# Three pairs of taps of four columns added on VectorE, sums of exponentials in three parts, and the last copy split between two engines

## The chip, the cores and the metric

The kernel runs on one core of a Trainium2 chip. The core has a TensorE (PE in the profile, with its weight loads apart as PEld), a VectorE (DVE), a ScalarE (ACT), a GpSimd (POOL) and a SyncE (SP); each works through its own queue in order and they wait for each other through semaphores. The metric is device microseconds of one execution, lower is better. The median of the three runs shown is 405.34 us (405.34 to 405.47).

## The reference

Two stages over 8 sequences of 4160 tokens with 192 features. The first is a convolution whose seven weights differ for each token and each of eight heads; they come out of a softmax. The second multiplies with two matrices, takes the larger of the two results for each hidden feature, and multiplies back.

```
w = exp(weight_gen - max); w = w / sum(w)            # over the 7 taps, per token and head
x_pad = [6 zero tokens, x]
y[b,s,h,:] = sum over k of w[b,s,h,k] * x_pad[b, s+k, head h]
g = maximum(y @ w1, y @ w2)                          # 192 -> 1024
out = g @ w_out                                      # 1024 -> 192
```

## The kernel before, in words

**Tiling.** The 33280 tokens lie 260 to a partition; a token's place in its partition is called a column. The columns are cut into 17 batches (16 columns each, then one of 12 and one of 8), and a batch into units of 4 columns (batches 0 and 1) or 8 (after them; the last few are smaller again). There are 38 units. A unit of 4 columns starting at column 8 of batch 1 is unit 6: columns 24 to 27 in the kernel's order, "1.8" in the steps below.

**The softmax** of a batch takes these steps: `exp_sum` (`X`, L153, ScalarE) takes the exponentials, `red` (`n`, L168, VectorE) sums seven of them for each token and head, `ln` (`l`, L172, ScalarE) takes the logarithm of the sums, `shift` (`s`, L177, VectorE) subtracts it from the weights, and `weights` (`W`, L191, ScalarE) takes the exponential again. `red`, `ln` and `shift` work on a whole batch or on one of several parts of it; `part` gives the columns.

**The convolution.** `mul` (`m`, L211, VectorE) multiplies a unit's columns, shifted by each of the seven taps, with the weights into `m_t`. For units from 8 on `adds` sums the seven products on VectorE in three instructions: three pairs of taps (L227), two pairs (L233), the last pair (L236, into `y_t`). A transposing DMA (L245, issued by SyncE) then gives `yt`, which TensorE reads. For units 0 to 7 VectorE adds nothing: `sum_transpose` (`y`, L281) lets TensorE sum and transpose all seven products with 64-wide matmuls against an identity matrix (2 x 7 x 6 = 84 matmuls), and `sums_out` (`e`, L293, ScalarE) copies the sums out.

**The second stage.** It uses max(a, b) = a + relu(b - a). `hid_tile` (L336, TensorE) makes tiles of hidden differences in PSUM, `relu` (L346, ScalarE) moves them to SBUF, `out_first` (L388 and L376) and `out_second` (L376) form the result of some columns (TensorE), and `evac` (L434, ScalarE) copies the result out. `relay` is a ScalarE instruction between `out_first` and `out_second`: the latter starts when ScalarE's queue has come to it.

**Order.** Up to about 47 us a list written out by hand, `OPENING`, sets the order of all engines' queues. From then on the work goes by groups of three hidden tiles, numbered from 8, and `hidden` writes each group in this order: TensorE makes tiles a and b and does `out_first`; ScalarE does relu a, relu b, the relay; TensorE makes tile c; `before()`; ScalarE does relu c; TensorE does `out_second`; ScalarE does `evac`; `after()`. What `before()` and `after()` put into ScalarE's queue stands in the table `SOFTMAX_AT`: the key (16, 1) with "l.5" means that the logarithm of batch 5 comes after the evac of group 16, and (44, 1), (72, 0) hold l.10 and l.15. This table is not touched by the change.

VectorE's queue is written by `extra`: while TensorE works on the second half of batch b, VectorE multiplies and adds the second half of batch b+1, and beside these adds come the sums of exponentials of batch b+3, through the callback `beside(i, 3)`, which `adds` calls ahead of each of its three instructions (i = 0, 1, 2). Beside the adds of a batch's first half comes the `shift` of the following batch, in three parts. The sums are in two parts before the change: ahead of the first and of the second add.

**PSUM and buffers.** From group 8 on there is one PSUM tile each for hidden tiles a, b and c and one ("r") for the results: `out_first` of a group waits for the `evac` of the group before.

**The end.** `rest_of_results` makes the last results; for the very last pair of columns `evac` copies 2 x 192 numbers with one ScalarE instruction (L422) and sends them out with two DMAs (L425), one issued by ScalarE, one by SyncE.

Of the kernel before, what the change touches and what calls it, by code (L numbers as in the profile page):

```python
# [9 lines left out]
FP32 = mybir.dt.float32  # L10
# [7 lines left out]
def _sub(base: bass.AP, off: int, dims):  # L18
    ap = [list(base.ap[0])] + [[int(s), int(c)] for s, c in dims]
    return dataclasses.replace(base, offset=base.offset + off, ap=ap)  # L20
# [3 lines left out]
def kernel(  # L24
# [9 lines left out]
    nc = tc.nc  # L34

    B, S, D = x.shape
    H, K = weight_gen.shape[2], weight_gen.shape[3]
    F = moe_w1.shape[1]
    P = 128
# [3 lines left out]
    HF = F // 2  # L43
# [8 lines left out]
    NB = len(BATCHES)  # L52

    def dcol(c):

        return (c + ROT) % CPP


    def pieces(b):
        n = BATCHES[b][1]  # L60
        at, done = [], 0
        for w in (4, 4, 4, 4) if b < 2 else (8, 8) if n == 16 else (8, 4) if n == 12 else (4, 4):
            at.append((done, w))
            done += w
        return at
# [14 lines left out]
    consts = ctx.enter_context(tc.tile_pool(name="consts", bufs=1))  # L80
# [76 lines left out]
    def part(b, i, of):  # L157

        n = BATCHES[b][1]
        c0, c1 = (4 * i, n if i else 4) if of == FIRST else (n * i // of, n * (i + 1) // of)  # L160
        h0, h1 = c0 * H, c1 * H
        return slice(h0, h1), h0 * K, [[K, h1 - h0], [1, K]]

    def red(b, i=0, of=1):
        if i == 0:
            s_ts[b] = psm.tile([P, BATCHES[b][1] * H], FP32, name="sum_t", tag="sum")
        hs, at, ap = part(b, i, of)
        nc.vector.reduce_sum(out=s_ts[b][:, hs], in_=_sub(e_ts[b], at, ap), axis=AX.X)  # L168
# [48 lines left out]
    def adds(b, o, first=False, beside=lambda i, of: None):  # L217


        w = dict(pieces(b))[o]  # L220
        n = w * D

        def taps(at, step, cnt):
            return _sub(m_t, K * o * D + at * n, [[step * n, cnt], [1, w * D]])

        beside(0, 3)
        nc.vector.tensor_tensor(out=taps(0, 1, 3), in0=taps(0, 1, 3), in1=taps(3, 1, 3), op=ALU.add)  # L227
        if first:
            return
        beside(1, 3)  # L230
        if b not in y_ts:
            y_ts[b] = py.tile([P, 16 * D], BF16, name="y_t", tag="y")
        nc.vector.tensor_tensor(out=taps(0, 2, 2), in0=taps(0, 2, 2), in1=taps(1, 5, 2), op=ALU.add)  # L233
        beside(2, 3)

        nc.vector.tensor_tensor(  # L236
            out=_sub(y_ts[b], o * D, [[64, 2], [P, 3 * w // 2], [1, 64]]),
            in0=taps(0, 1, 1), in1=taps(2, 1, 1), op=ALU.add,
        )
# [24 lines left out]
    def half(j):  # L264
        return slice(64 * j, 64 * j + 64)


    LEFT = (0, 1, 2, K - 1)

    def sum_transpose(u, i=None):  # L270

        b, o, n = UNITS[u]
        assert n == 4
        to = "h" if i == 0 else "o"
        yps = yps_of[u, i] = ps[to].tile([P, 1024], FP32, name="yps", tag="hd" if i == 0 else "op")
        ks = range(6) if i is None else range(3 * i, 3 * i + 3)
        for k in ks:
            for t in range(K):
                at = K * o * D + (t * 6 + k if i is None else (K * i + t) * 3 + k % 3) * P
                for r in range(2):  # L280
                    nc.tensor.matmul(  # L281
                        yps[:, r * 512 + k * 64:r * 512 + (k + 1) * 64],
                        lhsT=m_t[half(r), at:at + P], rhs=ident[half(r), half(r)],
                        start=(k == ks[0] and t == 0), stop=(t == K - 1),
                        skip_group_check=True,
                    )
# [69 lines left out]
    def place(p):  # L356

        u, i, _ = column(2 * p)
        b, o, n = UNITS[u]
        return BATCHES[b][0] + o + i, n // 2  # L360
# [55 lines left out]
    def evac(p, n):  # L416

        tile_, at = op_at[p]
        o = o_t[0]
        if p == NT // 2 - 1:  # L420

            nc.scalar.copy(out=_sub(o_last, 0, [[D, 2], [1, D]]),  # L422
                           in_=_sub(tile_, at, [[512, 2], [1, D]]))
            for j, eng in enumerate((nc.scalar, nc.sync)):
                eng.dma_start(  # L425
                    out=bass.AP(tensor=out.tensor, offset=dcol(place(p)[0] + 2 * j) * D, ap=[[CPP * D, P], [1, D]]),
                    in_=o_last[:, j * D:(j + 1) * D],
                )
            return
        runs = [[q for q in range(p, p + n) if column(2 * q)[0] == u]  # L430
                for u in range(column(2 * p)[0], column(2 * (p + n - 1))[0] + 1)]
        for qs in runs:
            c, h = place(qs[0])
            copied = nc.scalar.copy(out=_sub(o, c % 24 * D, [[D, len(qs)], [h * D, 2], [1, D]]),  # L434
                           in_=_sub(tile_, at + (qs[0] - p) * D, [[D, len(qs)], [512, 2], [1, D]]))
        stores = []
        for q in range(p, p + n):
            u, i, _ = column(2 * q)
            if u == NU - 2 and UNITS[u][2] == 8 and i % 2:
                stores.append((nc.sync, place(q)[0] - 1, [4 * D, 2], [1, 2 * D]))  # L440
            elif u < NU - 1 and i == UNITS[u][2] // 2 - 1:
                w = i + 1
                for k in range(0, 2 * w, w if u in PARTED else 2 * w):
                    stores.append((nc.sync, place(q)[0] - i + k, [1, (w if u in PARTED else 2 * w) * D]))
            if u == NU - 1:
                stores.append((nc.sync, place(q)[0], [2 * D, 2], [1, D]))
        for eng, c, *ap in stores:

            def issue(eng=eng, c=c, ap=ap, o=o):
                eng.dma_start(  # L450
                    out=bass.AP(tensor=out.tensor, offset=dcol(c) * D, ap=[[CPP * D, P], *ap]),
                    in_=_sub(o, c % 24 * D, ap),
                )

            if 3 <= u < NU - 3:
                held.append(issue)
            else:
                while u > 3 and held:
                    held.pop(0)()
                issue()  # L460
        return copied
# [9 lines left out]
    for g in range(3, len(GROUPS)):  # L471
        most = 4 if g == 3 else 2 if GROUPS[g][1] == 2 or len(OUTS[-1]) == 4 else 4
        n = min(most, ready[g] - c)
# [69 lines left out]
    ident, swap = around[:, 0:P], around[:, 64:64 + P]  # L543
    zeros = consts.tile([P, PAD * D], BF16, name="zeros")
    gate = consts.tile([P, 1], FP32, name="gate")
    o_last = consts.tile([P, 2 * D], FP32, name="o_last")

    pstage = ctx.enter_context(ExitStack())
    stage = pstage.enter_context(tc.tile_pool(name="pstage", bufs=1))
# [2 lines left out]
    ws = {(kind, wi): stage.tile([P, w], FP32, name=f"ws{wi}{kind}") for kind, w in (("E", F), ("T", HF)) for wi in range(2)}  # L552
# [10 lines left out]
    def load_w(h, wi):  # L563

        wsrc = (moe_w1, moe_w2)[wi]
        return nc.sync.dma_start(
            out=ws["E", wi][:, h * HF:(h + 1) * HF],
            in_=bass.AP(tensor=wsrc.tensor, offset=h * HF, ap=[[F, P], [1, HF]]),
        )

    def load_last(h, wi):

        wsrc = (moe_w1, moe_w2)[wi]
        return nc.sync.dma_start(  # L574
            out=ws["T", wi][half(h), :],
            in_=bass.AP(tensor=wsrc.tensor, offset=P * F + h * HF, ap=[[F, 64], [1, HF]]),
        )
# [124 lines left out]
    def results_buffer(_):  # L702
# [22 lines left out]
        e.0.1 d.0 d.2 t.0 k.3 t.2 T.3 d.1 T.4 h.0 h.1 t.1 X.1 r.0 lx.0.8.4 T.1 lo.0 r.1 m.0.4 n.1 v.0 h.2  # L725
        lx.1.0.8 V.1 y.1 r.2 l.1 h.3 e.1 m.0.8 lg.2@l.1 s.1 V.0 m.0.12 r.3 h.4 W.1.0 m.1.0 y.2 h.5 r.4 p.0
        e.2 r.5 h.6 lx.1.8.8@r.4 lg.3@e.2 y.3 W.1.8 h.7 lh.2 C.1 C.0 C.2 A.3 W.1.4 X.2 r.6 e.3 B.3 m.1.4 h.8
        D.3 y.4 r.7 r.8 Z.0 E.3 n.2 X.3 l.2 m.1.8 A.4 e.4 W.1.12 lx.2.0.8.0@r.7 B.4 h.9 D.4 h.10 r.9 E.4 s.2
        r.10 lg.4@r.9 y.5 W.2.0 A.5 h.11 B.5 h.12 e.5 D.5 n.3 r.11 r.12 A.6 m.1.12 E.5 h.13 B.6 D.6 y.6 r.13
        E.6 h.14 e.6 l.3 lx.2.8.8@r.13 h.15 r.14 A.7 W.2.8 B.7 y.7 D.7 r.15 e.7 E.7  # L730
    """

    make_identity(nc, ident_f)
# [28 lines left out]
    def extra(t):  # L762

        u, k = TILES[t]
        b, o, n = UNITS[u]
        s = o + k

        if s == 0 and b + 1 < NB:
            mul(b + 1, 0)
        later = 0 if b < 4 else 5  # L770
        if s == later and b + 1 < NB:

            c = b + 1
            adds(c, 0, beside=lambda i, of: shift(c + 1, i, of) if c + 1 < NB else None)
        if s == 8 and b + 2 < NB:
            mul(b + 1, 8)
        if s == 8 + later and b + 2 < NB:
            adds(b + 1, 8, beside=lambda i, of: red(b + 3, i, 2) if b + 3 < NB and i < 2 else None)
        if s == 8 and b + 2 == NB:
            mul(b + 1, 4)  # L780
            adds(b + 1, 4)
        if k == n // 4 - 1 and 7 < u + 1 < NU:
            transpose(u + 1)

    def steps(g, tiles):

        for t in tiles:
            extra(t)
# [36 lines left out]
```

## Time and profile before

| what | us |
|---|---|
| median of three runs | 405.34 |
| the profiled execution's own time | 405.37 |
| span of its profile | 403.6 |
| TensorE busy in matmuls | 394.8 (98%) |
| VectorE busy | 369.1 (91%) |
| ScalarE busy | 360.9 (89%) |
| granted TensorE clock | 1.0 |
| ScalarE waits for VectorE's sums of exponentials | 0.2, once, at 5.4 |
| TensorE sums and transposes unit 6 | 41.97 to 43.19 |
| the last copy (L422) starts | 400.05 |
| its DMAs are issued; they land | 400.56; 402.42 and 402.59 |

The busy share of an engine says how much of the span it has an instruction running; it does not say whether the others wait for it. The timeline gives each instruction's start and duration in microseconds from the start of the span; consecutive records of one engine overlap by about 0.1 us, so what an instruction costs in a full queue is the distance between starts.

### The profile page before, as it was taken

The page shows a single profiled execution, that of the slowest core. Times are in us where ns is not written, and L with a number is a line of the kernel's source. Part 1 is how long each engine was busy: PE and PEld are TensorE (multiplying, and loading weights), DVE is VectorE, ACT ScalarE, POOL GpSimd, SP SyncE. Part 2 cuts the span into 40 slices and gives each one's busy share as a digit, 9 for nine tenths or more (in the row PEclk, how much of TensorE's full clock was granted, in tenths as well). Part 3 has the DMA queues.
Part 4 walks back from the last instruction along what each step waited for, and adds up shares of the span by engine and source line. Part 5 has one row for each costly group of instructions (what it writes and reads, how often), then busy time and mean ns, then how long its engine had stood idle before and what let it go on. Part 6 is the DMA issues. An engine that isn't in the chain of part 4 may idle for free.

```text
span 403.6 us, 16321 instructions
## 1 busy us (share of the span) xinstructions
PE 394.8 (98%) x7499; PEld 321.3 (80%) x7499; DVE 369.1 (91%) x211; ACT 360.9 (89%) x466; POOL 72.3 (18%) x96
## 2 busy tenths in 40 slices
PE   7799999999999999999999999999999999999996
PEld 3589999777778777778777778877777877787996
DVE  5999999999999999999999999999999999998200
ACT  5999899999999989999899999989999899888872
POOL 3111031211122210222220122122012121200000
PEclk9999999999999999999999999999999999999999
DMA  8956468767768646864766667777457847558304
GB/s 262 222 140 151 120 124 167 183 164 133 190 110 222 182 79 129 240 187 80 217 187 107 141 192 193 99 215 198 81 115 228 178 80 200 141 106 193 104 31 169
DMA packets 60883, 63.16 MB, mean 157 GB/s; under 512 B 47641, under 2 KB 48665, under 8 KB 60816
## 3 DMA queue, kind: packets, MB, share of 16 engines
q1 hardware_dynamic: 52816, 40.15, 36.4%
q0 software_dynamic: 7856, 21.89, 27.4%
q8 instruction: 58, 0.95, 1.0%
q10 hardware_dynamic: 144, 0.10, 0.1%
q14 instruction: 9, 0.07, 0.1%
HBM read 36.55 MB, written 25.56 MB: 154 GB/s over the span
## 4 chain that ended last, share of the span: by engine, by line
PE 92%; ACT 5%; DMA 1%; SPq 1%; issue 0%
PE op_ps L376 42%; PE hdc L336 13%; PE hdb L336 13%; PE hda L336 13%; PE op_ps L388 8%; ACT rd_t L346 2%; DMA ws0E<-in_moe_w_dram 1%; PE hdp L336 1%; PE yps L281 1%; ACT en_t L191 1%; ACT yt L293 1%; ACT e_t L153 0%; ACT w1t L644 0%; SPq L574 0%; ACT w L622 0%
## 5 line engine op out<-in xcount | busy, mean ns | idle before, releaser
L376 PE MATMUL op_ps<-wo,rd_t 64*128 64x192 bf16 x4160 | 210.6, 243 | 0.0
L376 PEld LDWEIGHTS <-rd_t 64*128 64x128 bf16 x4160 | 181.0, 94 | 14.7
L211 DVE TENSOR_TENSOR m_t<-xb,en_t 128x10752 bf16<-128x10752 bf16 (+2 forms) x39 | 187.8, 4821 | 1.5 <-ACT en_t L191 1.4
L336 PEld LDWEIGHTS <-wd 64*128 64x128 bf16 x1824 | 96.8, 94 | 40.4 <-issue 2.5
L346 ACT ACTIVATE rd_t<-hdc 128x1024 bf16<-128x1024 f32 x82 | 84.1, 1025 | 17.8 <-PE hdc L336 16.2
L253 POOL CAST gate<-yt 128x1 f32<-128x1 bf16 x30 | 39.9, 1332 | 271.3 <-DMA yt<-y_t 271.3
L346 ACT ACTIVATE rd_t<-hda 128x1024 bf16<-128x1024 f32 x81 | 83.4, 1030 | 0.2 <-ACT o_t L434 0.2
L346 ACT ACTIVATE rd_t<-hdb 128x1024 bf16<-128x1024 f32 x81 | 83.5, 1031 | 0.0
L227 DVE TENSOR_TENSOR m_t<-m_t 128x4608 bf16<-128x4608 bf16 (+1 forms) x30 | 73.0, 2433 | 0.1
L336 PE MATMUL hdc<-yt,wd 64*128 64x512 bf16 (+1 forms) x552 | 67.9, 353 | 0.0
L434 ACT COPY o_t<-op_ps 128x384 f32<-128x384 f32 (+1 forms) x99 | 56.1, 577 | 12.4 <-PE op_ps L376 12.3
L336 PE MATMUL hdb<-yt,wd 64*128 64x512 bf16 (+1 forms) x540 | 67.1, 355 | 0.0
L336 PE MATMUL hda<-yt,wd 64*128 64x512 bf16 (+1 forms) x540 | 67.1, 355 | 0.0
L388 PE MATMUL op_ps<-w,yt 64*128 64x192 bf16 x780 | 55.5, 243 | 0.0
L388 PEld LDWEIGHTS <-yt 64*128 64x128 bf16 x780 | 39.0, 94 | 14.5 <-issue 0.3
L233 DVE TENSOR_TENSOR m_t<-m_t 128x3072 bf16<-128x3072 bf16 (+1 forms) x30 | 50.2, 1674 | 0.1
L191 ACT ACTIVATE en_t<-wg_t 128x896 bf16<-128x896 f32 (+3 forms) x48 | 35.7, 773 | 3.0 <-PE op_ps L376 2.0
L236 DVE TENSOR_TENSOR y_t<-m_t 128x1536 bf16<-128x1536 bf16 (+1 forms) x30 | 27.5, 916 | 0.6
L177 DVE TENSOR_TENSOR wg_t<-wg_t,sum_t 128x280 f32<-128x280 f32 (+6 forms) x46 | 22.2, 483 | 0.0
L168 DVE TENSOR_REDUCE sum_t<-e_t 128x64 f32<-128x448 f32 (+3 forms) x31 | 19.7, 639 | 2.3 <-ACT e_t L153 2.3
L125 POOL DMA_DIRECT2D xb<-in_x_dram x34 | 18.2, 537 | 17.3 <-ACT rd_t L346 11.0
L153 ACT ACTIVATE e_t<-wg_t 128x896 f32<-128x896 f32 (+2 forms) x18 | 15.9, 886 | 2.1 <-DMA wg_t<-in_weight_gen_dram 2.1
(40 smaller groups left out, 110.0 us busy)
## 6 DMA issues: line engine op xcount, KB each, us to landing
out_dram<-o_t SPq DMA_DIRECT2D x21, 768.0 KB, 4.3
xb<-in_x_dram POOLq DMA_DIRECT2D x30, 384.0 KB, 5.0
out_dram<-o_t SPq DMA_DIRECT2D x22, 384.0 KB, 3.7
wg_t<-in_weight_gen_dram POOLq DMA_DIRECT2D x13, 448.0 KB, 5.7
xb<-xb POOLq DMA_DIRECT2D x7, 288.0 KB, 5.1
wg_t<-in_weight_gen_dram SPq DMA_DIRECT2D x2, 448.0 KB, 5.2
xb<-in_x_dram POOLq DMA_DIRECT2D x4, 192.0 KB, 6.4
xs<-in_x_dram SPq DMA_DIRECT2D x1, 576.0 KB, 4.3
```

What stands on the lines that cost most here:

```text
L177: nc.vector.tensor_tensor(out=w_t, in0=w_t, in1=_sub(s_ts[b], hs.start, [[1, hs.stop - hs.start], [0, K]]), op=ALU.subtract)
L191: act = nc.scalar.activation(out=_sub(en_ts[b], (o * WGC + ((i or 0) * J + j) * N * K) * 2, [[2 * N, K], [2, N], [1, 2]]), in_=_sub(wg_ts[ ...
L211: return nc.vector.tensor_tensor(out=m_out, in0=x_in, in1=_sub(en_ts[b], at * H * 2, [[2, K * n * H], [0, G // 2], [1, 2]]), op=ALU.mult,)
L227: nc.vector.tensor_tensor(out=taps(0, 1, 3), in0=taps(0, 1, 3), in1=taps(3, 1, 3), op=ALU.add)
L233: nc.vector.tensor_tensor(out=taps(0, 2, 2), in0=taps(0, 2, 2), in1=taps(1, 5, 2), op=ALU.add)
L236: nc.vector.tensor_tensor(out=_sub(y_ts[b], o * D, [[64, 2], [P, 3 * w // 2], [1, 64]]), in0=taps(0, 1, 1), in1=taps(2, 1, 1), op=ALU.add,)
L253: nc.gpsimd.tensor_copy(out=gate, in_=yt[:, 0:1])
L336: nc.tensor.matmul(hid_out(t, f, j), lhsT=wd_at(j, s, f // 4, f % 4 * P, P), rhs=_sub(yt_ts[u][half(j), :], (s + j) % 3 * P, [[3 * P, w // ...
L346: relu_of[t0] = nc.scalar.activation(out=rd[:, k * 1024:(k + n) * 1024], in_=hd[:, at:at + n * 1024], func=AF.Relu)
L376: return nc.tensor.matmul(op_out(c), lhsT=rd[rows, k * 1024 + at:k * 1024 + at + P], rhs=wo[rows, f * D:(f + 1) * D], start=False, stop=(r ...
L388: nc.tensor.matmul(op_out(c + j), lhsT=yt_ts[u][half(j), (3 * i + (s + j) % 3) * P:(3 * i + (s + j) % 3 + 1) * P], rhs=w10[half(j), s * D: ...
L434: copied = nc.scalar.copy(out=_sub(o, c % 24 * D, [[D, len(qs)], [h * D, 2], [1, D]]), in_=_sub(tile_, at + (qs[0] - p) * D, [[D, len(qs)] ...
```

## The change

Four things, in the order of the kernel's text:

- Unit 6: `OPENING` has a new step `a.1.8` behind `m.1.8`. It is `adds` with `first=True`: one VectorE instruction adds taps 3 to 5 to taps 0 to 2 for four columns. The unit is noted in `fewer`, and `sum_transpose` then lets TensorE sum four products (taps 0, 1, 2 and 6) in place of seven: 48 matmuls in place of 84.
- The last pair of columns: ScalarE copies the first 192 numbers, VectorE the second 192, each into its own tile, and each DMA waits for its own copy.
- The sums of exponentials beside the adds of a batch's second half come in three parts (5, 5 and 6 columns of 16) ahead of the three adds, in place of two parts (8 and 8) ahead of the first two.
- `load_w` and `load_last` get forms (both halves at once; an issue by ScalarE) that no step of `OPENING` calls.

```diff
@@ adds
         nc.vector.tensor_tensor(out=taps(0, 1, 3), in0=taps(0, 1, 3), in1=taps(3, 1, 3), op=ALU.add)
         if first:
+            fewer.add((b, o))
             return
@@ sum_transpose
+        taps = (0, 1, 2, K - 1) if (b, o) in fewer else range(K)
         for k in ks:
-            for t in range(K):
+            for t in taps:
@@ evac, the last pair of columns
-            nc.scalar.copy(out=_sub(o_last, 0, [[D, 2], [1, D]]),
-                           in_=_sub(tile_, at, [[512, 2], [1, D]]))
-            for j, eng in enumerate((nc.scalar, nc.sync)):
+            for j, (eng, copy) in enumerate(((nc.scalar, nc.scalar.copy), (nc.sync, nc.vector.tensor_copy))):
+                copy(out=o_last[j], in_=tile_[:, at + 512 * j:at + 512 * j + D])
                 eng.dma_start(
...
-                    in_=o_last[:, j * D:(j + 1) * D],
+                    in_=o_last[j],
@@ OPENING
-        D.3 y.4 r.7 r.8 Z.0 E.3 n.2 X.3 l.2 m.1.8 A.4 e.4 W.1.12 lx.2.0.8.0@r.7 B.4 h.9 D.4 h.10 r.9 E.4 s.2
+        D.3 y.4 r.7 r.8 Z.0 E.3 n.2 X.3 l.2 m.1.8 a.1.8 A.4 e.4 W.1.12 lx.2.0.8.0@r.7 B.4 h.9 D.4 h.10 r.9
+        E.4 s.2 r.10 lg.4@r.9 y.5 W.2.0 A.5 h.11 B.5 h.12 e.5 D.5 n.3 r.11 r.12 A.6 m.1.12 E.5 h.13 B.6 D.6
@@ extra
-            adds(b + 1, 8, beside=lambda i, of: red(b + 3, i, 2) if b + 3 < NB and i < 2 else None)
+            adds(b + 1, 8, beside=lambda i, of: red(b + 3, i, 3) if b + 3 < NB else None)
```

More of the change, by code (lines that the diff above doesn't have):

```diff
@@ L265, in half @@
         return slice(64 * j, 64 * j + 64)
-    LEFT = (0, 1, 2, K - 1)
+    fewer = set()
     def sum_transpose(u, i=None):
@@ L545 @@
     gate = consts.tile([P, 1], FP32, name="gate")
-    o_last = consts.tile([P, 2 * D], FP32, name="o_last")
+    o_last = [consts.tile([P, D], FP32, name=f"o_last{j}") for j in range(2)]
     pstage = ctx.enter_context(ExitStack())
@@ L565, in load_w, with load_last @@
         wsrc = (moe_w1, moe_w2)[wi]
+        at, w = (0, F) if h == 2 else (h * HF, HF)
         return nc.sync.dma_start(
-            out=ws["E", wi][:, h * HF:(h + 1) * HF],
-            in_=bass.AP(tensor=wsrc.tensor, offset=h * HF, ap=[[F, P], [1, HF]]),
+            out=ws["E", wi][:, at:at + w],
+            in_=bass.AP(tensor=wsrc.tensor, offset=at, ap=[[F, P], [1, w]]),
         )
-    def load_last(h, wi):
+    def load_last(h, wi, act=0):
         wsrc = (moe_w1, moe_w2)[wi]
-        return nc.sync.dma_start(
+        return (nc.scalar if act else nc.sync).dma_start(
             out=ws["T", wi][half(h), :],
@@ L727 @@
         e.2 r.5 h.6 lx.1.8.8@r.4 lg.3@e.2 y.3 W.1.8 h.7 lh.2 C.1 C.0 C.2 A.3 W.1.4 X.2 r.6 e.3 B.3 m.1.4 h.8
-        D.3 y.4 r.7 r.8 Z.0 E.3 n.2 X.3 l.2 m.1.8 A.4 e.4 W.1.12 lx.2.0.8.0@r.7 B.4 h.9 D.4 h.10 r.9 E.4 s.2
-        r.10 lg.4@r.9 y.5 W.2.0 A.5 h.11 B.5 h.12 e.5 D.5 n.3 r.11 r.12 A.6 m.1.12 E.5 h.13 B.6 D.6 y.6 r.13
-        E.6 h.14 e.6 l.3 lx.2.8.8@r.13 h.15 r.14 A.7 W.2.8 B.7 y.7 D.7 r.15 e.7 E.7
+        D.3 y.4 r.7 r.8 Z.0 E.3 n.2 X.3 l.2 m.1.8 a.1.8 A.4 e.4 W.1.12 lx.2.0.8.0@r.7 B.4 h.9 D.4 h.10 r.9
+        E.4 s.2 r.10 lg.4@r.9 y.5 W.2.0 A.5 h.11 B.5 h.12 e.5 D.5 n.3 r.11 r.12 A.6 m.1.12 E.5 h.13 B.6 D.6
+        y.6 r.13 E.6 h.14 e.6 l.3 lx.2.8.8@r.13 h.15 r.14 A.7 W.2.8 B.7 y.7 D.7 r.15 e.7 E.7
     """
```

## The prediction

> **What bounds the kernel now.** I read the page first, its busy shares and the chain that ended last.
>
> ```profile
> span 403.6 us, 16321 instructions
> ...
> PE 394.8 (98%) x7499; PEld 321.3 (80%) x7499; DVE 369.1 (91%) x211; ACT 360.9 (89%) x466; POOL 72.3 (18%) x96
> ...
> PE 92%; ACT 5%; DMA 1%; SPq 1%; issue 0%
> ```
>
> The reader is to see that TensorE is the bound: the chain runs on it for 92% of the span, and from about 30 us on it has no gap. So a matmul less is time won, and any wait that TensorE gets anew is time lost for good. The other two engines are at 89% and 91%, so neither has much room to make up a delay. Then the waits, for ScalarE's logarithms, since the change moves what they read.
>
> ```profile
> ACT sum_t L172 <- DVE sum_t L168: 0.2, 1, 0.2
> ```
>
> Of 18 logarithms only one ever waited for VectorE's sums, the one at 5.4 us. By the timelines the others have room, but unequal room: the change is decided there. Batch 5 has the least, on VectorE and on ScalarE:
>
> ```profile
> 80.20 0.61 DVE L168 TENSOR_REDUCE sum_t<-e_t 128x64 f32<-128x448 f32 x1
> 80.73 2.55 DVE L227 TENSOR_TENSOR m_t<-m_t 128x4608 bf16<-128x4608 bf16 x1
> 83.20 0.62 DVE L168 TENSOR_REDUCE sum_t<-e_t 128x64 f32<-128x448 f32 x1
> 83.72 1.75 DVE L233 TENSOR_TENSOR m_t<-m_t 128x3072 bf16<-128x3072 bf16 x1
> 85.51 0.96 DVE L236 TENSOR_TENSOR y_t<-m_t 128x1536 bf16<-128x1536 bf16 x1
> 86.39 5.75 DVE L211 TENSOR_TENSOR m_t<-xb,en_t 128x10752 bf16<-128x10752 bf16 x1
> ```
>
> ```profile
> 84.64 0.31 ACT L172 ACTIVATE sum_t<-sum_t 128x128 f32<-128x128 f32 x1
> 84.85 1.02 ACT L346 ACTIVATE rd_t<-hda 128x1024 bf16<-128x1024 f32 x1
> 85.75 1.03 ACT L346 ACTIVATE rd_t<-hdb 128x1024 bf16<-128x1024 f32 x1
> 86.75 1.02 ACT L346 ACTIVATE rd_t<-hdc 128x1024 bf16<-128x1024 f32 x1
> 87.67 0.47 ACT L434 COPY o_t<-op_ps 128x384 f32<-128x384 f32 x1
> ```
>
> The second part of the sums ends at 83.82 and l.5 starts at 84.64: 0.82 us of room. Behind l.5 in ScalarE's queue stand the relus, the relay and the evac of group 17, and TensorE waits for those.
>
> **The change part by part.**
>
> *Fewer matmuls.* In the chain the 84 matmuls of unit 6 take 1.22 us (41.97 to 43.19), 14.5 ns each. 36 go: 36 x 14.5 = 0.52 us. ScalarE's copy of these sums waits for them today (idle 0.49 ahead of it at 43.23), so ScalarE comes forward too, and the work up to 84 us moves forward by 0.52 on both engines. What is late next is looked at below.
>
> *The new add* (2304 numbers per partition). The same form stands near the end, behind a multiplication of the same size:
>
> ```profile
> 357.13 2.96 DVE L211 TENSOR_TENSOR m_t<-xb,en_t 128x5376 bf16<-128x5376 bf16 x1
> 360.12 1.36 DVE L227 TENSOR_TENSOR m_t<-m_t 128x2304 bf16<-128x2304 bf16 x1
> ```
>
> The multiplication holds the queue for 2.99 when the add needs its result, against 2.87 today (m.1.8 at 31.32, s.2 at 34.19). The add holds it for 1.36 less the 0.08 by which an independent successor starts early: 1.28. Together 2.99 - 2.87 + 1.28 = **1.40 us**, at 34 us. VectorE has no idle row from there to 363 us, so nothing swallows it: everything on VectorE comes 1.40 later. Near at hand this is covered: y.6 needs the add by 41.3, it is there at 35.6; W.2.0 starts at 36.90 and s.2 will end at 36.67; l.3 and m.2.0 have over 3 us and 2 us. The transposes have room too: the landing of `yt` leads its first matmul by 13.5 us at unit 8, falling to 1.6 at unit 30 (315.92 against 317.49). With the forecast below this lead does not go under 2 us.
>
> *Sums in three parts.* Sizes of 280, 280 and 336 numbers: the reduction rows give 0.38 for 224, 0.50 for 336, 0.62 for 448, so 0.44, 0.44 and 0.50. What the queue makes of three such pieces is shown by the subtractions, which are already in three parts of the same size:
>
> ```profile
> 68.39 0.44 DVE L177 TENSOR_TENSOR wg_t<-wg_t,sum_t 128x280 f32<-128x280 f32 x1
> ...
> 73.25 0.50 DVE L177 TENSOR_TENSOR wg_t<-wg_t,sum_t 128x336 f32<-128x336 f32 x1
> ...
> 74.53 5.75 DVE L211 TENSOR_TENSOR m_t<-xb,en_t 128x10752 bf16<-128x10752 bf16 x1
> ```
>
> From the first part to the next multiplication it is 74.53 - 68.39 = 6.14, against 86.39 - 80.20 = 6.19 with two sums: a third piece costs nothing, since it fills the pause between two adds of which one reads the other (the third add starts 0.04 behind its predecessor's end where nothing lies between, 0.08 ahead of the end where something does). So VectorE gains 0.05 a batch. The Trainium skill says otherwise ("VectorE: DVE Perf Modes", Rules for kernel authors): it advises a minimum of operations, since each waits for the pipe of the one before to empty; by that rule the time would be the second rival's. This trace does not agree: 6.14 with three pieces, 6.19 with two. But the third part ends much later: 73.75 - 68.39 = 5.36 behind the start of the first, where the second of two ends 3.62 behind it.
>
> *What that does to l.5.* One batch of sums (batch 4) comes before, so VectorE is 1.40 - 0.05 = 1.35 late. First part at 80.20 + 1.35 = 81.55, third ends at 86.91, logarithm 0.04 later (5.38 behind 5.34 in the one wait there is): **86.95**. ScalarE would be there at 84.64 - 0.52 = 84.12 and waits 2.83 us. Behind it, by start distances: logarithm 0.21, relu a 0.90, relu b 0.91, relu c 0.90, evac 0.47, and 0.05 to the matmul that needs the evac (smallest distance in the trace, 79.85 to 79.90): 86.95 + 3.44 = 90.39. That matmul is `out_first` of group 18:
>
> ```profile
> 86.53 0.84 PE L376 MATMUL op_ps<-wo,rd_t 64*128 64x192 bf16 x16
> 87.19 0.83 PE L336 MATMUL hda<-yt,wd 64*128 64x512 bf16 x6
> 87.84 0.83 PE L336 MATMUL hdb<-yt,wd 64*128 64x512 bf16 x6
> 88.48 0.43 PE L388 MATMUL op_ps<-w,yt 64*128 64x192 bf16 x6
> ```
>
> It started at 88.48, so TensorE is 90.39 - 88.48 = **1.91 us later than before** from there on; the 0.52 is gone, and 1.91 on top. Part of this TensorE loses a little earlier, where `out_second` (86.53) waits for the relay, but that is the same time, not more. Then relu c of group 18 waits for TensorE again, as before, and ScalarE is back in step.
>
> *The later logarithms* with TensorE 1.91 late and VectorE 1.40 less 0.05 a batch: l.8 is ready at 151.20 + 1.20 + 5.40 = 157.80 and due at 159.81; l.10 ready at 198.53 + 1.10 + 5.40 = 205.03, due at 205.16; l.12 252.27 against 254.26; l.15 (parts of 4 columns, 5.13) at 316.87 + 0.85 + 5.17 = 322.89 against 322.81, with 0.9 of room behind it. None adds anything.
>
> *The last copy.* ScalarE's rows are 0.48 for 2 x 192 numbers and 0.80 for 768, so 192 take about 0.32. VectorE copying 192 from PSUM has no row; VectorE's nearest are 0.38 (224 numbers, subtraction) and 0.76 (1152, cast), below stands 0.27 (112): I take 0.35, ends 0.27 and 0.76. The DMAs leave 0.13 to 0.16 earlier: **-0.15**, ends -0.2 and +0.3. Nothing else is in VectorE's queue then.
>
> *The load functions* gain forms that no step calls: nothing.
>
> **Sum** against the profiled execution (405.37, span 403.6; the median is 0.03 lower): -0.52 + 2.43 - 0.15 = +1.76 us, so 405.34 + 1.76 = **407.1**.
>
> **The rivals.**
>
> *The logarithm is not late (not slower).* Behind l.5 there is 88.48 - 84.64 - 3.44 = 0.40 of room, so if the third part is ready by 85.04, or 85.19 with the shorter end, the kernel is not slower. For that VectorE would have to swallow the new add somewhere between 34 and 80 us. Against it: no idle row there, and the third part alone, without the add, ends at 80.20 - 0.05 + 5.36 = 85.51. Then the time is 85.55 + 3.44 - 88.48 - 0.15 = +0.36: 405.7. If ScalarE's wait vanished wholly, -0.67: 404.7.
>
> *Each operation costs its whole length.* Then three sums take 1.38 against 1.23: +0.15 a batch in place of -0.05, and some 0.12 more to the end of the third. l.5 is ready at 80.20 + 1.55 + 5.52 = 87.27, TensorE 2.23 late; l.10 at 198.53 + 2.30 + 5.52 = 206.35 against 205.48, 0.87 late with 0.41 of room, TensorE 2.69 late; l.15 at 316.87 + 3.05 + 5.29 = 325.21 against 323.59, 1.62 late with 0.94 of room, TensorE 3.37 late: 408.6. The rows of the three subtractions speak against it. This is the case that the page's rule would give.
>
> *A second logarithm adds to the first.* l.10 is on time by 0.13 only; with VectorE 0.3 to 1 later than I reckon, it and l.15 eat their room: 407.6 to 408.3.
>
> **How the numbers follow.** Forecast (406.6 to 407.6) 0.72; a second logarithm 0.09; whole length 0.06; add swallowed (405.7) 0.08; no lateness (404.7, a little less if the end gains more) 0.05. The range leaves out the last, the whole-length case and the far end of the second logarithm: 405.6 to 408.0. A measurement of this kernel can tell about 0.2% (0.8 us) from no change: faster by more 0.03 (the best end of the last case), within 0.10 (the rest of it and the swallowed add), slower by more 0.87.
>
> **What would show it.** In the waits, a line of ScalarE's L172 for L168 with one wait near 2.8 us, just after an evac near 84; the third reduction ending near 86.9; TensorE's first real gaps between 86 and 91 us, 2.4 in all; L281 down from 672 to 636 matmuls; the new add at 34 us with 1.36; no further gap of TensorE to the end. I am wrong if L172 does not wait there, if TensorE's gaps are under 1.5 us, or if a later logarithm makes gaps of its own.

## The result and the profile after

The changed kernel takes 408.9 us (median of six runs, 407.76 to 410.14), the kernel before 405.4 beside it (405.17 to 407.17): ratio 1.0081, 95% interval 1.0058 to 1.0104. It is slower, as forecast, and by about twice as much: the forecast was 407.1, the range ended at 408.0. The profiled execution took 408.36 us with a span of 406.5.

First the page of the kernel after: span, busy shares, and the chain that ended last.

```profile
span 406.5 us, 16263 instructions
...
PE 396.2 (97%) x7463; PEld 320.1 (79%) x7463; DVE 370.7 (91%) x226; ACT 360.2 (89%) x466; POOL 176.5 (43%) x96
...
DVE 41%; PE 35%; DMA 9%; issue 8%; ACT 6%; SPq 1%; POOL 0%; DVEq 0%; POOLq 0%
```

Two things stand out. TensorE carried 92% of the chain and now carries 35%, VectorE 41%: TensorE waits for what VectorE delivers. And GpSimd's busy time, which the prediction did not look at, went from 72.3 to 176.5 us with the same 96 instructions. The groups show which of them; the columns are busy time and mean ns of one. Kernel before:

```profile
L253 POOL CAST gate<-yt 128x1 f32<-128x1 bf16 x30 | 39.9, 1332 | 271.3 <-DMA yt<-y_t 271.3
```

Kernel after:

```profile
L254 POOL CAST gate<-yt 128x1 f32<-128x1 bf16 x30 | 144.2, 4808 | 172.3 <-DMA yt<-y_t 172.2
```

This `gate` is a copy of one number per partition from a transposed tile. It has no use as data: it stands in `transpose` so that GpSimd issues the loads of `x` behind it only once the transpose has landed. The change doesn't touch it. Thirty copies, 104 us more.

The waits of the kernel after (total us, times, longest):

```profile
ACT sum_t L172 <- DVE sum_t L168: 5.8, 4, 2.7
DVE m_t L211 <- DMA xb<-xb: 1.8, 2, 1.0
```

The first line was forecast, but with one wait, not four. The second is new: VectorE's multiplications wait for loads of `x`.

**Where TensorE lost the time.** Set against each other hidden tile by hidden tile, TensorE's starts in the two traces differ by

| from (us, before) | after less before | what ends the new gap there |
|---|---|---|
| 43.0 (behind unit 6) | -0.50 | fewer matmuls |
| 89.4 (group 18) | +1.90 | logarithm of batch 5 |
| 209.0 | +2.30 | logarithm of batch 10 |
| 324.8 | +3.00 | logarithm of batch 15 |

and by nothing over 0.1 elsewhere; each step has built up within the 3 us before the time given. From the start of the last matmul to the end of the span it is 3.74 in place of 3.80. The first two rows are the forecast to 0.02; the last two were not in it.

### The profile page after: what moved, and what is told of

It reads as the page before. It is cut to its first block, busy times and chain, and to the rows that moved or that the text cites. A ratio compares the mean times of both kernels' runs of the same rounds, so it can differ in the third digit from the quotient of the medians.

```text
span 406.5 us, 16263 instructions
## 1 busy us (share of the span) xinstructions
PE 396.2 (97%) x7463; PEld 320.1 (79%) x7463; DVE 370.7 (91%) x226; ACT 360.2 (89%) x466; POOL 176.5 (43%) x96
## 4 chain that ended last, share of the span: by engine, by line
DVE 41%; PE 35%; DMA 9%; issue 8%; ACT 6%; SPq 1%; POOL 0%; DVEq 0%; POOLq 0%
DVE m_t L211 18%; PE op_ps L378 16%; DVE m_t L227 10%; DVE m_t L234 7%; PE hdc L338 5%; DMA xb<-xb 4%; PE hda L338 4%; PE hdb L338 4%; PE op_ps L390 3%; DVE y_t L237 3%; DMA yt<-y_t 3%; ACT rd_t L348 3%; DVE wg_t L177 2%; DVE sum_t L168 2%; DMA ws0E<-in_moe_w_dram 1%
## 5 line engine op out<-in xcount | busy, mean ns | idle before, releaser
L254 POOL CAST gate<-yt 128x1 f32<-128x1 bf16 x30 | 144.2, 4808 | 172.3 <-DMA yt<-y_t 172.2
L227 DVE TENSOR_TENSOR m_t<-m_t 128x4608 bf16<-128x4608 bf16 (+1 forms) x31 | 74.3, 2395 | 0.1
L168 DVE TENSOR_REDUCE sum_t<-e_t 128x40 f32<-128x280 f32 (+6 forms) x44 | 21.5, 490 | 2.3 <-ACT e_t L153 2.3
```

The lines of the kernel that those rows point to most:

```text
L254: nc.gpsimd.tensor_copy(out=gate, in_=yt[:, 0:1])
```

## The experiments

Theory 1 came out of these traces. The third part of the sums fills the only pause in VectorE's queue; without it GpSimd's copy is shut out for up to 13.6 us, the loads behind it leave late, VectorE waits for `x`, and with that the logarithms of batches 10 and 15 come late. The logarithm of batch 5 is late besides, by the order of the program alone, as forecast. The other theories are named in each expectation.

One held copy shows what theory 1 is about. GpSimd in the kernel after:

```profile
92.88 12.40 POOL L254 CAST gate<-yt 128x1 f32<-128x1 bf16 x1 [7.36 <-DMA yt<-y_t]
105.22 0.53 POOL L125 DMA_DIRECT2D xb<-in_x_dram  x1
```

VectorE in the same stretch:

```profile
98.61 0.95 DVE L237 TENSOR_TENSOR y_t<-m_t 128x1536 bf16<-128x1536 bf16 x1
99.48 5.75 DVE L211 TENSOR_TENSOR m_t<-xb,en_t 128x10752 bf16<-128x10752 bf16 x1
105.15 0.44 DVE L168 TENSOR_REDUCE sum_t<-e_t 128x40 f32<-128x280 f32 x1
```

The copy starts at 92.88, when its transpose has landed, and ends at 105.28. In between VectorE runs eight instructions with two inputs each, every one starting before its predecessor has ended; the copy gets in only when a reduction, which has one input, starts at 105.15. In the kernel before the copy of the same unit came at 90.33 and was through at 92.18, as the multiplication ended:

```profile
90.33 1.85 POOL L253 CAST gate<-yt 128x1 f32<-128x1 bf16 x1 [8.98 <-DMA yt<-y_t]
```

There, of 30 copies none took over 1.85 us; here nine take 10.3 to 13.6. And in the kernel before, the rows of batch 5 in the prediction show the pause: 83.72 + 1.75 = 85.47, the third add starts at 85.51.

### The rest of the change, without the three parts (e1)

The changed kernel with the sums in two parts:

```diff
-            adds(b + 1, 8, beside=lambda i, of: red(b + 3, i, 3) if b + 3 < NB else None)
+            adds(b + 1, 8, beside=lambda i, of: red(b + 3, i, 2) if b + 3 < NB and i < 2 else None)
```

> The changed kernel with the sums of exponentials back in two parts; the new add and the split copy stay. Theory 1 (the third sum fills the only pause in VectorE's queue, GpSimd's one-number copies behind the transposes then find no place, the loads of x come late, VectorE waits, and the logarithms of batches 10 and 15 are late): GpSimd's copies are short again (about 1.3 us each, none above 3), VectorE waits for no load before 360 us, l.5 is ready at 83.82 + 1.40 + 0.04 = 85.26 and costs TensorE 88.70 - 88.48 = +0.2 against before, l.10 and l.15 cost nothing: 405.5 us. Theory 2 (the loads are late because VectorE is 1.4 us later and its loads meet other transfers): waits of VectorE and late later logarithms stay, 406.6 us.

Measured: 406.26 us against 405.92, ratio 1.0010 (1.0001 to 1.0020). GpSimd is busy for 73.1 us, no copy over 1.86, and VectorE waits for no load of `x` before 360 us. TensorE: -0.58 behind unit 6, then +0.75 at batch 5's logarithm, then +0.30 at unit 30, where it waits for the transposed tile. By time alone the run lies between the two theories (405.5 and 406.6), so the trace has to decide: short copies, no late loads, no late later logarithms. Most of the loss comes with the third part; and even without it the new add eats more than its matmuls give.

### The three parts alone (e2)

The kernel before with only the third part, the opposite edit of the same line:

```diff
-            adds(b + 1, 8, beside=lambda i, of: red(b + 3, i, 2) if b + 3 < NB and i < 2 else None)
+            adds(b + 1, 8, beside=lambda i, of: red(b + 3, i, 3) if b + 3 < NB else None)
```

> The kernel before with the sums in three parts and nothing else. Theory 1: GpSimd's copies get long (several above 10 us), VectorE waits for x once or more, l.5 is ready at 80.20 - 0.05 + 5.40 = 85.55 (+0.5 for TensorE), l.10 and l.15 add up to 1.0 more: 406.9 us, between 405.9 and 407.5, with more spread than before. Theory 2: no waits of VectorE, only l.5: 405.9 us, and copies of about 1.3 us.

Measured: 408.46, ratio 1.0071 (1.0055 to 1.0087): above both expectations. The mechanism is the one of theory 1: GpSimd busy for 177.8 us, nine copies of 12 to 13.6. But VectorE waits longer here than in the changed kernel (1.39 at 135.7, where the load that it needs lands at 135.60, and 2.59 at 280.0), since other copies are the held ones, and TensorE loses 1.09 by 209 and 2.25 by 325. Theory 2 falls with this: here VectorE has no new add and the waits are there, in e1 it has the add and they are not. What a held copy costs depends on which load stands behind it; the expectation had carried over the losses of the changed kernel. The trace is that of the slowest of the six executions (409.71), so its losses are larger than those of the median.

### The copy replaced (e3, e9, e10, e11)

If the copy is what is held up, the same order of transfers without it should bring the forecast's time back. In e3 an empty GpSimd instruction waits for the transpose in its place (`landed` is the transposing DMA issued just above it):

```diff
-        nc.gpsimd.tensor_copy(out=gate, in_=yt[:, 0:1])
+        tc.add_manual_dep(nc.gpsimd.nop().ins, landed.ins.name, SYNC, reason="its place among the transfers")
```

> The changed kernel with GpSimd's one-number copy behind each transpose replaced by an empty GpSimd instruction that waits for the same transpose and reads nothing. Theory 1: loads of x leave right after each transpose, VectorE never waits for x before 360 us, only l.5 costs: +1.9 for TensorE, 407.2 us, little spread. Theory 2: as the changed kernel, 408.4 to 408.9 us.

Measured: 407.38, ratio 1.0042 (1.0029 to 1.0054), as expected. No wait of VectorE for `x`; TensorE's only new gaps are those of batch 5's logarithm (+2.40 in all). The kernel of e9 keeps an instruction that touches SBUF, but only writes:

```diff
-        nc.gpsimd.tensor_copy(out=gate, in_=yt[:, 0:1])
+        tc.add_manual_dep(nc.gpsimd.memset(gate, 0.0).ins, landed.ins.name, SYNC, reason="its place among the transfers")
```

> The changed kernel, but GpSimd's one-number copy, which reads the transposed tile, becomes a write of zero into the same number; it waits for the same transpose and only then releases the loads of x. Theory 1 (what is held up is the copy's reading of SBUF while VectorE's two-input instructions follow each other without a pause): a write that reads nothing gets through, GpSimd is busy well under 40 us in place of 176.5, VectorE has no wait for x, and the time is that of the kernel without a copy at all, 407.4 (407.1 to 407.8). Rival (any GpSimd instruction that touches SBUF is shut out while VectorE's queue has no pause): waits of 10 to 13 us remain, GpSimd is busy for over 150 us, and the time is 408.4 to 408.9.

Measured: 407.28, ratio 1.0031 (1.0007 to 1.0055). GpSimd in the stretch shown above:

```profile
92.14 0.10 POOL L254 MEMSET gate<- 128x1 f32 x1 [10.72 <-DMA yt<-y_t]
92.65 0.53 POOL L125 DMA_DIRECT2D xb<-in_x_dram  x1 [0.41 <-issue]
```

0.10 us in place of 12.40, beside the same VectorE queue without a pause. The load behind shows the same, apart from how long the profile makes a GpSimd row: it leaves at 92.65 in place of 105.22. So it is the reading that is shut out, not every instruction of GpSimd. TensorE's shift in this trace is -0.48, then +1.92 from group 18 to the end, without a further step: the forecast's own sum, with its cause isolated. The Trainium skill ("SBUF — State Buffer", Who interferes with whom) says that VectorE and GpSimd share a pair of ports as an exclusive lock, that a VectorE instruction with two SBUF inputs contends with a GpSimd instruction that reads SBUF, and that a reduction never does. The traces agree on who contends (a copy held for 12.40, a write through in 0.10, copies let in at reductions). The same page of the Trainium skill (section SBUF: two separate sides) has the loser shut out for one whole instruction of the other; here the copy above stayed out past the ends of seven instructions in a row.

> The kernel before with the sums in three parts as its only edit of the work, and with an empty GpSimd instruction (it waits for the transpose, reads and writes nothing) in place of the one-number copy. The three parts with the copy measured 408.46, ratio 1.0071. Theory 1 (most of that is the copy held up by a VectorE queue without a pause): what is left is the third part that comes late for l.5, worked out in the prediction as +0.36 with a 0.15 from the last copy that is not here, so about +0.5: 406.0 (405.6 to 406.4), VectorE without a wait for x. Rival (the third part itself costs three times as much, since sums that come late delay the logarithms of each batch): 407.5 to 408.5 whatever GpSimd does.

This is e2 with the empty instruction. Measured: 405.98 us against 405.49, ratio 1.0004 (0.9982 to 1.0025), against 1.0071 with the copy. TensorE loses 0.49 at batch 5's logarithm and nothing else. The third part costs what the prediction's first rival had for it (0.36, with 0.15 off for a last copy that is not here); the rest of e2's loss goes away with the copy.

> The kernel before with the empty GpSimd instruction in place of the one-number copy and no other edit. In the kernel before every copy takes 0.49 to 1.85 us and no load of x is late. Theory 1: with no hold-up to remove, nothing is gained: 405.4, within 0.3 of the kernel before, and the empty instruction itself costs nothing, so the runs that use it can be read against the kernel before. Rival (the copies cost something even where they are short, by the ports that they share with VectorE): 404.5 to 405.0.

The control, the kernel before with the empty instruction: 405.95 us against 405.49, ratio 0.9999 (0.9975 to 1.0023). Where the copies were short, no gain or loss clear of the scatter is seen, which here is up to 1 us. In its profiled execution TensorE is 0.51 later by 17 us already, and stays so; such a start also shifts e3's trace (by 1.30). It comes ahead of the first copy (55 us) and of the new add (34 us), so it isn't due to the edits.

### The pause given back (e4, e8)

e4 is the changed kernel with the first two parts ahead of the first add and the third ahead of the second, so that nothing lies between the second add and the third:

```diff
+            adds(b + 1, 8, beside=lambda i, of: [red(b + 3, j, 3) for j in ((0, 1), (2,), ())[i]] if b + 3 < NB else None)
```

> The changed kernel with the sums still in three parts, but the first two ahead of the first add and the third ahead of the second, so that nothing stands between the second and the third add. Theory 1: the pause is there, GpSimd's copies are short, VectorE does not wait for x; the third sum ends 3.69 behind the start of the first, l.5 is ready at 85.39, TensorE +0.35: 405.7 us. Rival (three pieces as such hold GpSimd up, wherever they stand): long copies and late later logarithms, 406.6 us.

Measured: 406.57, ratio 1.0015 (1.0007 to 1.0024). Three parts as before, 0.04 us of pause a batch, and no copy takes over 1.85 (GpSimd busy for 75.0). The time is 0.9 above what I expected, but not for the rival's reason, which was long copies. TensorE starts 0.47 late in the trace, and its new gaps are 0.57 at 47 us, 0.29 at batch 5's logarithm, and 0.26 and 0.20 where it waits for transposed tiles at 317 and 363; the one at 47, before the first sums beside the adds come into play, can't be derived from the edit and stays unexplained.

e8 puts the pause into the other half instead, where the subtractions stand, and leaves the sums in three parts:

```diff
-            adds(c, 0, beside=lambda i, of: shift(c + 1, i, of) if c + 1 < NB else None)
+            adds(c, 0, beside=lambda i, of: shift(c + 1, i, 2) if c + 1 < NB and i < 2 else None)
```

> The changed kernel with the subtractions beside the adds of a first half in two parts in place of three, so that VectorE's queue has a pause between second and third add there, and none beside the sums. Theory 1 (any pause lets a waiting copy in): no GpSimd copy takes more than about 6 us, since the pause comes 5.2 us behind the end of the multiplication; VectorE waits for no x load; only l.5 costs (ready 87.05, +2.0): 407.3 us. Rival (the pause has to come just ahead of the multiplication that the copy waits for): copies above 10 us as in the changed kernel, 408.4 to 408.9 us.

GpSimd in e8:

```profile
93.49 5.74 POOL L254 CAST gate<-yt 128x1 f32<-128x1 bf16 x1 [7.42 <-DMA yt<-y_t]
```

VectorE in e8:

```profile
97.44 1.75 DVE L234 TENSOR_TENSOR m_t<-m_t 128x3072 bf16<-128x3072 bf16 x1
99.22 0.96 DVE L237 TENSOR_TENSOR y_t<-m_t 128x1536 bf16<-128x1536 bf16 x1
```

The second add ends at 99.19, the third starts at 99.22, and the copy ends at 99.23: it got in at the pause. All 13 copies that are held in this way end there; the longest takes 6.94. That is theory 1's mechanism at the place where it was put. The time was the rival's all the same: 408.9, ratio 1.0079 (1.0067 to 1.0091). The loads now leave just ahead of the transpose of a batch's first half. These transposes land 5.0 to 8.5 us behind their add up to unit 34, in the kernel before 3.8 to 5.0, and TensorE waits for transposed tiles at 317 (+0.94) and 363 (+0.61). That is 1.55 of the 4.01 by which TensorE ends late; batch 5's logarithm has 1.37, a start as in e4 0.47, and a gap at 47 us, as e4 has one, 1.15, unexplained here too; unit 6 gives 0.53 back. A pause that lets the copy in is not enough; the loads must also leave at a harmless time.

### The logarithms later (e5, e6, e7)

Five logarithms are moved behind the next evac or half a group on, so that none waits:

```diff
-(16, 1): "l.5",  (34, 0): "l.8",  (44, 1): "l.10", (45, 1): "W.9.8",  (56, 0): "l.12",  (72, 0): "l.15",
+(17, 1): "l.5",  (34, 1): "l.8",  (45, 1): "l.10 W.9.8",              (56, 1): "l.12",  (72, 1): "l.15",
```

> The changed kernel with the logarithms of batches 5, 8, 10, 12 and 15 put 0.5 to 1 group later in ScalarE's queue (l.5 behind the evac of group 17, l.8, l.12 and l.15 behind the relu c and evac of their own group, l.10 behind the evac of group 45). GpSimd's copies are as in the changed kernel. If the late logarithms are the only way in which the change loses time: 404.8 us. Theory 1 (GpSimd's late copies still make VectorE late, by up to 2.9 us near unit 30, where yt leads its first matmul by only 1.57 us before): no ScalarE wait for the sums of batch 5, but TensorE then waits for yt near units 30 to 33 by 2.9 - 0.5 ahead - 1.57, up to 1.8 in all: 405.5 to 406.7 us.

Measured: 411.07, ratio 1.0128 (1.0112 to 1.0144). Missed by far: it is slower than the changed kernel. Its waits (total us, times, longest):

```profile
DVE m_t L211 <- DMA xb<-zeros: 9.5, 1, 9.5
PE hda L338 <- DMA yt<-y_t: 3.0, 3, 1.4
...
PE hdc L338 <- DMA yt<-y_t: 1.6, 1, 1.6
```

The waits for the five logarithms are gone (GpSimd is still busy for 172.2 us), and TensorE, which is earlier now, runs into the late loads itself, by way of VectorE and the transposed tiles: four gaps from 143 to 340 us leave it 2.94 behind the kernel before, about what the logarithms cost in the changed kernel (3.00). Two more, 1.73 at 381 and 1.56 at 386, make it 6.24. They follow VectorE's wait for the load `xb<-zeros`, which lands at 376.03. In the changed kernel it lands at 373.38, and a wait of 7.7 us for it costs TensorE nothing. The held copy ahead of this load ends 0.9 us later in e5; the rest of the 2.65 lies in slower transfers, for which no run here shows the reason.

e6 does the same with the empty instruction in place of the copy, e7 with the copy and the sums in two parts.

> The logarithms later as in the run before, and GpSimd's copies replaced by an empty instruction that reads nothing. Theory 1: nothing of the loss is left, TensorE is 0.5 earlier, VectorE about 0.85 later at unit 30, lead of yt 1.57 - 0.85 - 0.5 = 0.2, no waits: 404.8 us (ratio 0.9985). Rival (something else in the change costs time, the add itself or the split copy): 405.4 or more.

> The logarithms later, the sums in two parts, GpSimd's copies as they are. The copies are short; VectorE is 1.4 later throughout, so that the lead of yt at unit 30 is 1.57 - 1.4 - 0.5 = -0.35: TensorE waits some 0.3 to 0.4 there: 405.1 us (ratio 0.9995). If the third sum had no use for VectorE (rival), there is no wait at unit 30: 404.8.

Measured: e6 405.52, ratio 0.9998 (0.9983 to 1.0013); e7 405.79, ratio 1.0007 (0.9995 to 1.0020). Both lie 0.7 above what was expected, and neither beats the kernel before. In e6 TensorE's shift is -0.26 until 317 and then +0.29, where it waits for the transposed tile of unit 30. Of the 0.5 that the matmuls give, nothing is left: at unit 30 VectorE is 0.92 later, by its new add, the transpose lands 5.52 behind its add in place of 4.63, and a lead of 1.57 is too little for both. No version here is faster than the kernel before by more than the scatter.

## Why the prediction was right in its direction and wrong in its size

*Fewer matmuls* (-0.52): at unit 6 TensorE gains 0.52 to 0.53 in all nine traces with this edit (the -0.50 of the table counts a start 0.02 late). Right.

*The new add* (VectorE 1.40 late): the next multiplication starts 1.41 later. Right, and nothing swallowed it. "The transposes have room" held where the rest of the forecast held: in e9, without held copies, the lead at unit 30 is 3.60. In the changed kernel it is 0.05, down from 1.57 and not over 2: with its waits for loads VectorE is 2.85 late there, and the transpose lands 5.63 behind its add in place of 4.63. That just costs nothing, as TensorE is late too; where TensorE is not, it waits there, 0.30 in e1 and 0.55 in e6.

*A third piece costs nothing on VectorE.* Right for VectorE itself. Its rows after:

```profile
81.55 0.44 DVE L168 TENSOR_REDUCE sum_t<-e_t 128x40 f32<-128x280 f32 x1
...
84.73 1.75 DVE L234 TENSOR_TENSOR m_t<-m_t 128x3072 bf16<-128x3072 bf16 x1
86.39 0.50 DVE L168 TENSOR_REDUCE sum_t<-e_t 128x48 f32<-128x336 f32 x1
...
87.67 5.75 DVE L211 TENSOR_TENSOR m_t<-xb,en_t 128x10752 bf16<-128x10752 bf16 x1
```

First part to next multiplication: 6.12, against 6.19 with two; the sums end at 86.89 (forecast 86.91). **This is the step that failed all the same.** "It fills the pause between two adds" was true, and the pause was booked as 0.05 us of VectorE's time. It was also where GpSimd came to read, and the prediction asked of no engine but VectorE what the pause was for. In place of nothing, filling it held GpSimd's copies for up to 13.6 us, made VectorE wait 1.90 for loads, and through that cost TensorE 0.40 and 0.70 at two later logarithms (1.5 to 1.6 us by the medians with and without the copy). The line of GpSimd stood on the page before (72.3 us for 96 instructions, 30 of them copies of a single number at 1.3 us each, where the shortest took 0.18: far too long for the work, so they were waiting for something while counted as busy).

*The logarithm of batch 5* (ready 86.95, TensorE +1.91): ScalarE and TensorE after:

```profile
86.92 0.31 ACT L172 ACTIVATE sum_t<-sum_t 128x128 f32<-128x128 f32 x1 [2.69 <-DVE sum_t L168]
```

```profile
87.12 0.83 PE L378 MATMUL op_ps<-wo,rd_t 64*128 64x192 bf16 x16 [0.91 <-ACTq L411]
...
90.39 0.42 PE L390 MATMUL op_ps<-w,yt 64*128 64x192 bf16 x6 [0.46 <-ACT o_t L435]
```

86.92, and `out_first` at 90.39, exactly the forecast's time. Following the queue behind a late instruction row by row gave a size right to 0.01.

*The later logarithms add nothing.* Wrong, as a consequence of the failed step. GpSimd, and VectorE behind it, at one of the places:

```profile
260.49 11.04 POOL L254 CAST gate<-yt 128x1 f32<-128x1 bf16 x1 [8.72 <-DMA yt<-y_t]
271.48 0.53 POOL L125 DMA_DIRECT2D xb<-in_x_dram  x1
272.00 0.55 POOL L139 DMA_DIRECT2D xb<-xb  x1
```

```profile
278.64 5.76 DVE L211 TENSOR_TENSOR m_t<-xb,en_t 128x10752 bf16<-128x10752 bf16 x1 [1.03 <-DMA xb<-xb]
```

The copy holds the loads until 271.5, they land at 278.5, VectorE waits 1.03. With 0.78 at 183.1 and 0.09 at 111.4 VectorE has waited 1.90 by batch 15, for which the forecast has nothing. Two logarithms show it on ScalarE:

```profile
205.98 0.31 ACT L172 ACTIVATE sum_t<-sum_t 128x128 f32<-128x128 f32 x1 [0.72 <-DVE sum_t L168]
...
324.87 0.28 ACT L172 ACTIVATE sum_t<-sum_t 128x96 f32<-128x96 f32 x1 [2.19 <-DVE sum_t L168]
```

l.10 at 205.98 in place of 205.03 costs TensorE 0.40, l.15 at 324.87 in place of 322.89 costs 0.70. This is the place and nearly the size of the third rival (VectorE 0.3 to 1 later than reckoned, 407.6 to 408.3; the two logarithms came 0.95 and 1.98 later than reckoned), which had a chance of 0.09 because no cause for a later VectorE had been looked for. The second rival, by which each operation costs its whole length, named the same two logarithms and nearly the time, for a reason that the rows refute (6.12).

*The last copy* (-0.15): -0.06. ScalarE and VectorE after:

```profile
403.05 0.32 ACT L425 COPY o_last<-op_ps 128x192 f32<-128x192 f32 x1
403.40 0.36 DVE L425 COPY o_last<-op_ps 128x192 f32<-128x192 f32 x1 [18.13 <-ACT o_last L425]
```

Both sizes were right (0.32 and 0.35); that they run at the same time was not. VectorE's copy is released by the end of ScalarE's, so its DMA leaves 0.39 behind the other (403.79 and 403.40).

Sum after, by these rows: -0.50 + 2.40 + 0.40 + 0.70 - 0.06 = +2.94, 405.37 + 2.94 = 408.31 against 408.36 profiled. The median of 408.9 lies 0.5 above that execution; single runs of this kernel differ by more than that, and the traces of the kernels here differ by up to 1.3 us at 17 us already. By the traces the held copies cost 1.1 us, by the medians with and without the copy 1.5 to 1.6; the difference can't be told from the scatter.

**What stays open.** In the kernel before, the pause comes once a batch, at 85.47, and the copy that arrives in the following multiplication is let in at that multiplication's end, 6.7 us later, between two instructions with two inputs each. In the changed kernel it isn't, at eight of the ten ends of the same kind; of the other two, one (the copy of 187.50) ends with the multiplication that VectorE began after waiting 0.78 for `x`. The eight traces that have the copy show how far a pause reaches. Take, up to 358 us, every end at which VectorE goes from one two-input instruction straight to the next while a copy waits. If VectorE had been idle for at least 0.02 us no more than three instructions (8.6 us) earlier, the copy got in at 62 of 63 such ends; if the last such pause lay nine instructions (18 us) or more back, at 2 of 238. Where VectorE started a reduction, it got in at 126 of 127. That the pause decides is shown by e1, e4, e8 and this count; why it still counts some instructions later is not. Open too are the gap at 47 us in e4 and e8, the slower transfers at the end of e5, and the 0.5 us between trace and median.

## What to carry to other kernels

A few hundredths of a microsecond of idle time in a full VectorE queue can decide for the next instructions whether GpSimd gets to read SBUF: before filling it, look at what GpSimd's short reads take, and whether loads are issued behind them. An instruction that is there only to order transfers should read nothing; a write or an empty instruction keeps the order, and neither was shut out here. And a piece of work that is moved costs what the first late consumer makes of it: follow that consumer's queue row by row, but also recheck every later consumer whose room is under half a microsecond against an error in the reckoning.

## What the runs showed of the hardware

- A one-number GpSimd copy out of SBUF took 0.18 to 1.9 us (once 2.6, in e7) beside a VectorE queue with one pause of 0.04 us a batch, and up to 13.6 us beside one without; a one-number write took 0.10 in the same place.
- The held copy was let in when VectorE started a reduction, or at a pause of 0.03 to 0.04 us, and could be passed over at seven ends of instructions in a row. Between two two-input instructions it got in at 62 of 63 ends with a pause up to three instructions back, at 2 of 238 with the last pause nine or more back.
- In e8, where loads leave just ahead of them, the transposes of first halves land 5.0 to 8.5 us behind their add; in the kernel before 3.8 to 5.0.
- Removing a wait can make a kernel slower: with the logarithms moved later the changed kernel went from 1.0081 to 1.0128, since TensorE, once earlier, lost 3.3 us at the late loads by 340 us and 3.3 more behind a load that landed 2.65 later than in the changed kernel.
